# First keys loaded as fp32 by SyncE and converted on chip, counters that write the frequencies, and ScalarE's sine table as its first

## The chip, the core and the metric

The kernel runs on one core of one Trainium2 chip. The core has five engines, each with its own in-order queue: TensorE (PE, matrix products; its weight loads are shown as PEld), VectorE (DVE), ScalarE (ACT), GpSimd (POOL) and SyncE (SP). PE writes to PSUM, the others work between PSUM and SBUF, and 16 DMA engines move data between the device's memory and SBUF. Here loads that convert fp32 to bf16 on the way are issued by POOL; SP issues plain copies and transposes. The metric is the time on the device in microseconds (us), as the median of several executions.

## The reference

Eight batches, eight heads, 576 positions of 64 values; the attention uses 128 random features, and its output goes through a gated convolution along the positions.

```python
def phi(x):                                   # x: q or k, scaled by 64 ** -0.25
    proj = np.einsum('bhsd,md->bhsm', x, omega)
    h = proj - np.sum(x * x, axis=-1, keepdims=True) / 2.0
    return np.exp(h - np.max(h, axis=-1, keepdims=True)) / np.sqrt(m)
kv = np.einsum('bhsm,bhsd->bhmd', k_p, v)
num = np.einsum('bhsm,bhmd->bhsd', q_p, kv)
den = np.einsum('bhsm,bhm->bhs', q_p, np.sum(k_p, axis=2))[..., None] + 1e-06
x = heads_joined(num / den)                   # (8, 576, 512)
proj = x @ w_proj                             # (512, 1536): x1, x2, x3
x2_conv = irfft(rfft(x2, axis=1) * rfft(filter_fft, axis=0), axis=1)
out = (x1 * x2_conv * x3) @ w_out             # (8, 576, 512) fp32
```

## The kernel before

Each batch has 512 main positions, four tiles of 128, and 64 left ones; the left ones of two batches share a tile. The attention of a batch turns keys and queries (`kn`, `qn`) with PE, so that the 64 values lie on partitions (`kt`, `qt`), multiplies them with omega (`om2`), and ACT takes the exponentials (`ek`, `eqt`; `ekl`, `eql` for left positions). A factor 1/max of each key goes into the values on DVE (`vc`, `vcl`), PE sums keys with values (`kv`), multiplies queries with it, DVE divides, and the result is turned into `xt`. Then comes the convolution: `fold` makes three combinations of `xt`, PE multiplies them with `wproj` (`project2`), a forward transform (`fwb`, `fwa`, `fwn`), a product with the transformed filter (`spectrum`), the gates x1 and x3, an inverse transform (`gtab`, `gta`, `gns`), and the product with `wout`. All 576 positions are seen as three chunks of 192 (`CH`), so a transform's length is 192 and the frequencies are of three classes.

The transform's tables are made on the chip at the start. `make_residues` (line 562) builds for each partition its frequencies `fr` on DVE, from a counter `pi` that POOL wrote as int32, along with signs `sg`, phases `ph` and masks `mk`; `fs` is `fr` / 576. A second counter `si` (tile `x2`) holds the positions 0 to 383 and is converted to fp32 in `sc` (tile `xf`). For three groups of columns ACT rounds position x frequency / 576 to a whole number (`yt`, an Identity with a scale per partition), DVE makes the remainder (`xt`, fp16) and, for the cosines, its absolute value with `scalar_tensor_tensor`. `sines` (line 666) has ACT take the five sines, into `gtab`, `gta` and `gn`; `tables` (line 683) turns them with PE. ACT holds one table of functions at a time: it loads that of exponentials first, that of sines ahead of the sines, and that of exponentials again.

Loads: SP issues omega; POOL issues every other load, the keys of batch 0 in two parts (`load_main(0, "k", 2, first_constants)`, line 492) with the counters and the identity for the turns between them, then queries, values, left positions, weights and, behind the residues, the filter, whose tiles `yt` are the residues' before.

The order of instructions is not the program's. `nc` is a `Plan`: each call is recorded with a cost (`_cost`, line 197) and a due time, which is worked out backwards from its users and from the constants `PERIOD`, `STRETCH`, `STAY`, `LEAD`, `SHIFT` and `LEAN` at the top; `simulate` (line 276) goes through a model of the engines and queues and issues, engine by engine, the ready call that is due first. So a change of any cost or constant can move every instruction. All instructions stand in the profile under line 390, where the plan issues them, and are told apart by their tiles.

Of the kernel before, what the change touches and what calls it, by code (L numbers as in the profile page):

```python
# [2 lines left out]

# [11 lines left out]
INT32 = mybir.dt.int32  # L15
# [7 lines left out]
PERIOD, STRETCH, STAY = 132.577, 8.076, 3059.83  # L23
LEAD = {
    "cross keys": -1.86, "cross out": 1.89, "cross queries": -0.95, "filter": -1.41,
    "fold": -1.38, "forward": 68.57, "gates": 0.52, "inverse": -1.95, "keys": 5.37,
    "left keys": -0.11, "left out": -0.33, "left queries": 37.06, "load filter": -63.41,
    "load k": -0.23, "load kl": -0.83, "load q": 0.19, "load ql": 1.42, "load v": 0.21,
    "load vl": -0.15, "load w0": -1.83, "load w1": 5.49, "load w2": 1.25, "out": -1.99,
    "queries": -0.43, "residues": 1.48, "rest": 0.66, "sines": 4.41, "start": -115.12,  # L30
    "sums": 37.58, "tables": -1.3, "turn out": -0.79, "turn queries": -0.04, "values": 96.58,
    "zeros": -0.01,
# [3 lines left out]
    ("fold", 0): -6.59, ("fold", 1): 51.34, ("forward", 1): -64.26, ("forward", 6): -65.11,  # L36
    ("forward", 7): -64.2, ("left keys", 2): 46.16, ("left queries", 7): -36.93,
    ("load kl", 0): -35.9, ("load q", 0): 1.17, ("load v", 0): -95.34, ("load v", 1): 95.91,
    ("load vl", 0): -20.54, ("out", 1): 148.99, ("queries", 1): 32.44, ("queries", 6): -10.06,
    ("rest", 1): 255.75, ("rest", 7): 5.08, ("sums", 2): -41.35, ("sums", 6): -35.91,  # L40
    ("sums", 7): -35.42, ("turn out", 1): 6.64, ("turn out", 2): -370.9,
    ("turn queries", 0): -3.89, ("turn queries", 2): 31.07, ("values", 0): -72.86,
    ("values", 1): 308.0, ("values", 2): -98.35,
}
LEAN = {
    ("fold", "DVE"): 3.25, ("forward", "PE"): 23.82, ("gates", "PE"): 78.43,
    ("keys", "PE"): -26.62, ("rest", "DVE"): 4.62, ("rest", "PE"): -3.97, ("start", "POOL"): 0.17,
    ("turn out", "DVE"): 4.04, ("turn queries", "DVE"): 13.21,
}

SIZE = {FP32: 4, INT32: 4, BF16: 2, FP16: 2, mybir.dt.uint32: 4}
# [58 lines left out]
class Plan:  # L110
# [86 lines left out]
    def _cost(self, op, eng, name, outs, ins):  # L197
# [6 lines left out]
        if name == "dma_start":  # L204
            a = out if out.space != bass.MemoryType.DRAM else ins[0]
            run = a.ap[-1][1] * SIZE[a.dtype]
            rows = a.ap[0][1] * self._free(a) // a.ap[-1][1]
            if eng == "POOL":
                op.busy, op.lat = (880.0 if rows > 600 else 720.0), 3300.0
                op.dma = ("SW", rows * max(run, 166) / 198.0)  # L210
            else:
                op.busy, op.lat = 580.0, 2000.0
                op.dma = ("HW", rows * run / 180.0 / (1 if out.space == bass.MemoryType.DRAM else 4))
            return
# [61 lines left out]
    def simulate(self):  # L276
# [16 lines left out]
        dma_free = {"SW": 0.0, "HW": 0.0}  # L293
        lanes = {"SW": [0.0] * 8, "HW": [0.0] * 8}
        for op in ops:
            if not op.deps:
                ready[op.eng].append(op)
        done, turn = [], {"SW": 0, "HW": 0}
        span, used, slow, half, table = 0, 0.0, True, False, "exp"
        while len(done) < len(ops):  # L300
# [46 lines left out]
            elif op.table and op.table != table:  # L347
                table = op.table
                busy, lat = busy + 1283.0, lat + 1283.0
            if op.dma:  # L350
                kind, serve = op.dma
                go = max(dma_free[kind], at + op.lat)
                if kind == "HW" and dma_free["SW"] > at:
                    go += 2500.0
                    if busy > 1000.0:
                        go, busy = go + 6000.0, busy + 4000.0
                dma_free[kind] = go + serve
# [36 lines left out]
def kernel(  # L394
# [87 lines left out]
    pi_ = nc.tile(const, [P, 1], INT32, name="pi")  # L482
    si = nc.tile(hy, [P, 1024], INT32, name="x2", bufs=2)

    def first_constants():
        was, nc.where = nc.where, ("start", 0)
        nc.gpsimd.iota(pi_[:], pattern=[[1, 1]], base=0, channel_multiplier=1)
        nc.gpsimd.iota(si[:, 0 : 2 * CH], pattern=[[1, 2 * CH]], base=0, channel_multiplier=0)
# [3 lines left out]
    load_main(0, "k", 2, first_constants)  # L492
# [69 lines left out]
    def make_residues():  # L562

        sc = nc.tile(hy, [P, 2 * CH], FP32, name="xf", bufs=2)
        pf_ = nc.tile(const, [P, 4], FP32, name="pf")
        fr = nc.tile(const, [P, 4], FP32, name="fr")
        fl = nc.tile(const, [P, 2], FP32, name="fl")
        sg = nc.tile(const, [P, 2], FP32, name="sg")
        ph = nc.tile(const, [P, 3], FP32, name="ph")
        mk = nc.tile(const, [P, 2], FP32, name="mk")  # L570
        ts, tt = nc.vector.tensor_scalar, nc.vector.tensor_tensor
        stt = nc.vector.scalar_tensor_tensor
        p_ = fr[:, 0:1]
        nc.vector.tensor_copy(out=p_, in_=pi_[:])

        ts(out=pf_[:, 1:2], in0=p_, scalar1=63.5, scalar2=None, op0=ALU.is_ge)
        stt(out=pf_[:, 2:3], in0=pf_[:, 1:2], scalar=-64.0, in1=p_, op0=ALU.mult, op1=ALU.add)
        ts(out=mk[:, 1:2], in0=pf_[:, 2:3], scalar1=31.5, scalar2=None, op0=ALU.is_ge)
        ts(out=mk[:, 0:1], in0=mk[:, 1:2], scalar1=-1.0, scalar2=1.0, op0=ALU.mult, op1=ALU.add)
        stt(  # L580
            out=pf_[:, 3:4],
            in0=mk[:, 1:2],
            scalar=-32.0,
            in1=pf_[:, 2:3],
            op0=ALU.mult,
            op1=ALU.add,
        )
        ts(out=fr[:, 1:2], in0=pf_[:, 2:3], scalar1=128.0, scalar2=None, op0=ALU.add)
        ts(out=fr[:, 2:3], in0=pf_[:, 2:3], scalar1=3.0, scalar2=None, op0=ALU.mult)
        ts(out=fr[:, 3:4], in0=pf_[:, 3:4], scalar1=3.0, scalar2=192.0, op0=ALU.mult, op1=ALU.add)  # L590
        ts(out=fl[:], in0=fr[:, 0:2], scalar1=0.5, scalar2=-0.25, op0=ALU.mult, op1=ALU.add)
        ts(out=fl[:], in0=fl[:], scalar1=MAGIC, scalar2=-MAGIC, op0=ALU.add, op1=ALU.add)
        nc.vector.scalar_tensor_tensor(
            out=fr[:, 0:2], in0=fr[:, 0:2], scalar=1.0, in1=fl[:], op0=ALU.add, op1=ALU.add
        )


        ge2 = pf_[:, 1:2].to_broadcast([P, 2])
        ts(out=sg[:], in0=ge2, scalar1=2.0, scalar2=-1.0, op0=ALU.mult, op1=ALU.add)
        ts(  # L600
            out=ph[:, 0:2],
            in0=ge2,
            scalar1=-math.pi / 2,
            scalar2=math.pi / 2,
            op0=ALU.mult,
            op1=ALU.add,
        )
        nc.vector.memset(ph[:, 2:3], math.pi / 2)
        nc.vector.memset(fr[64:65, 2:3], 288.0)
        nc.vector.memset(sg[64:65, 1:2], -1.0)  # L610
        nc.vector.memset(ph[64:65, 1:2], math.pi / 2)
        zb = nc.tile(const, [P, 1], FP32, name="zb")
        nc.vector.memset(zb[:], 0.0)
        mg = nc.tile(const, [P, 1], FP32, name="mg")
        nc.vector.memset(mg[:], MAGIC)
# [932 lines left out]
```

## Time and profile before

| | us |
|---|---|
| median of three runs | 268.56 |
| the three runs | 266.85, 269.07, 268.56 |
| the profiled execution | 267.76 |
| its span, first to last instruction | 265.8 |
| PE busy | 239.2 (90%) |
| DVE busy | 214.7 (81%) |
| ACT busy | 193.9 (73%) |
| POOL busy | 62.6 (24%) |

The granted TensorE clock was 1.000. The span is what the profile covers; the execution's time has another 1.96 us around it. Busy PE is not PE at its peak, since matrix products overlap and their ends are modelled. The profile's timeline gives for each group its start, its busy time, the engine, the operation, `out<-in` by the names of tiles, and in brackets the idle time ahead of it with what ended it. POOLq and SPq stand for those engines' queues that issue DMAs.

### The profile page before, as it was taken

The numbers are of one execution on the slowest core, as the hardware profiler recorded it, in microseconds if no ns is written. First come the engines' busy times: TensorE is split into PE (matmuls) and PEld (weight loads), VectorE is DVE, ScalarE is ACT, GpSimd is POOL, SyncE is SP. The second block draws the span as 40 slices with busy tenths as digits, with TensorE's granted clock in tenths as the row PEclk, the third lists the DMA queues.
The fourth block names the chain that finished last, engine by engine and source line by source line (L and its number), as shares of the span: only waits on it lengthen the run. The fifth ranks groups of instructions, "written<-read, shape, count | busy, mean of one in ns | idle before, by whom it ended". The sixth has DMA issues, their size and how long they took to land.

```text
span 265.8 us, 5693 instructions
## 1 busy us (share of the span) xinstructions
PE 239.2 (90%) x2202; PEld 133.9 (50%) x2202; DVE 214.7 (81%) x481; ACT 193.9 (73%) x304; POOL 62.6 (24%) x86
## 2 busy tenths in 40 slices
PE   0375879999999998998999599999999999999994
PEld 0264547555466465454854254544664554455541
DVE  7889985678888989998889595999979993576880
ACT  1897898469998989987557548996669647746433
POOL 8745633544453534410230000000000000000000
PEclk9999999999999999999999999999999999999999
DMA  6999999999999999799599727743418053302306
GB/s 78 189 196 176 192 219 221 181 168 163 143 160 147 185 154 100 168 171 217 125 154 167 153 59 194 106 158 91 89 36 244 4 108 129 81 20 64 136 0 197
DMA packets 93026, 36.83 MB, mean 139 GB/s; under 512 B 64459, under 2 KB 87496, under 8 KB 93000
## 3 DMA queue, kind: packets, MB, share of 16 engines
q0 software_dynamic: 59616, 17.31, 64.5%
q1 hardware_dynamic: 33240, 19.04, 32.8%
q8 instruction: 17, 0.28, 0.4%
q10 hardware_dynamic: 144, 0.13, 0.1%
q14 instruction: 9, 0.07, 0.1%
HBM read 34.64 MB, written 9.44 MB: 166 GB/s over the span
## 4 chain that ended last, share of the span: by engine, by line
PE 73%; DMA 11%; ACT 6%; DVE 6%; issue 3%; SPq 0%; ACTq 0%; DVEq 0%
PE h L390 58%; PE a L390 11%; DMA yt<-in_moe_filter_fft_dram 5%; DMA out_dram<-osb 5%; PE t L390 4%; ACT eqt L390 2%; ACT osb L390 1%; DVE yt L390 1%; DMA xw<-xr 1%; DVE x L390 1%; DVE vc L390 1%; SPq L390 0%; ACT yt L390 0%; DVE xt L390 0%; DVE vcl L390 0%
## 5 line engine op out<-in xcount | busy, mean ns | idle before, releaser
L390 PE MATMUL h<-xt,wproj 128*128 128x512 bf16 x256 | 61.7, 380 | 0.0
L390 ACT CAST x<-h 128x512 bf16<-128x512 f32 x68 | 40.2, 600 | 24.7 <-PE h L390 23.4
L390 PEld LDWEIGHTS <-wproj 128*128 128x128 bf16 x384 | 31.0, 99 | 26.3 <-issue 2.3
L390 ACT ACTIVATE osb<-h 128x512 f32<-128x512 f32 (+4 forms) x49 | 27.6, 567 | 11.5 <-PE h L390 6.9
L390 ACT ACTIVATE ek<-a 128x1024 bf16<-128x1024 f32 x32 | 32.1, 1047 | 2.6 <-PE a L390 2.5
L390 ACT ACTIVATE eqt<-a 128x1024 bf16<-128x1024 f32 x32 | 32.6, 1051 | 1.2 <-PE a L390 1.1
L390 PE MATMUL h<-wproj,xf 128*128 128x512 bf16 x128 | 31.4, 380 | 0.0
L390 PE MATMUL h<-wout,yt 128*128 128x512 bf16 x128 | 30.9, 379 | 0.3 <-DVE yt L390 0.3
L390 DVE TENSOR_TENSOR x<-h,x 128x512 bf16<-128x512 f32 x32 | 21.9, 685 | 7.3 <-PE h L390 4.3
L390 POOL DMA_DIRECT2D qn<-in_q_dram x26 | 22.9, 892 | 14.1 <-PE t L390 5.1
L390 PEld LDWEIGHTS <-yt 128*128 128x128 bf16 x128 | 12.2, 98 | 14.8 <-DVE yt L390 0.8
L390 PE MATMUL h<-x,fwb 128*128 128x512 bf16 x72 | 18.5, 379 | 0.9 <-ACT osb L390 0.9
L390 PE MATMUL h<-gtab,xs 128*128 128x384 bf16 x64 | 15.6, 325 | 3.6 <-ACT osb L390 2.2
L390 PEld LDWEIGHTS <-xf 128*128 128x128 bf16 x134 | 12.4, 100 | 12.7 <-issue 0.5
L390 DVE TENSOR_TENSOR bt<-h,osb 128x384 f16<-128x384 f32 x32 | 16.9, 552 | 1.6 <-ACT osb L390 0.7
L390 DVE TENSOR_TENSOR xf<-xt 128x1024 bf16<-128x1024 bf16 (+1 forms) x16 | 8.7, 552 | 7.5 <-ACT xt L390 4.5
L390 PEld LDWEIGHTS <-eqt 128*128 128x128 bf16 x256 | 11.2, 98 | 4.9 <-DVE xb L390 0.7
L390 DVE TENSOR_TENSOR xb<-a,rden 128x512 bf16<-128x512 f32 x20 | 13.2, 678 | 0.3
L390 PE MATMUL a<-om,kt 64*128 64x128 bf16 x256 | 11.8, 223 | 1.5 <-ACT ek L390 0.8
L390 PE MATMUL a<-qt,om 64*128 64x512 bf16 x64 | 11.3, 383 | 1.8 <-DVE qt L390 1.2
L390 POOL DMA_DIRECT2D vn<-in_v_dram x8 | 7.2, 902 | 23.3 <-DVE x13l L390 13.5
L390 PE MATMUL a<-kv,eqt 128*128 128x65 bf16 x256 | 12.5, 194 | 0.0
(168 smaller groups left out, 469.0 us busy)
## 6 DMA issues: line engine op xcount, KB each, us to landing
out_dram<-osb SPq DMA_DIRECT2D x24, 256.0 KB, 2.4
vn<-in_v_dram POOLq DMA_DIRECT2D x8, 512.0 KB, 9.0
kn<-in_k_dram POOLq DMA_DIRECT2D x7, 512.0 KB, 7.3
qn<-in_q_dram POOLq DMA_DIRECT2D x24, 128.0 KB, 9.7
sw<-sp SPq DMA_DIRECT2D x16, 128.0 KB, 2.4
wproj<-in_moe_w_proj_dram POOLq DMA_DIRECT2D x3, 512.0 KB, 13.0
qn<-in_q_dram POOLq DMA_DIRECT2D x2, 512.0 KB, 9.9
out_dram<-xf SPq DMA_DIRECT2D x4, 256.0 KB, 2.0
```

The costliest lines, as they stand in the source:

```text
L390: getattr(real, name)(*args, **kw)
```

## The change

The keys' main part of batch 0 is loaded as fp32 in two DMAs which SP issues, into a tile that takes one of the two `ek` buffers; DVE converts four heads to bf16 and ACT the other four. The counters write fp32 directly: 1 + 3 x partition, and for each half of the partitions 385 + 3 x partition and 3 x partition (within the half); a fourth column adds 192 or 96. These are the frequencies `fi`, so the steps that derived them from a partition's number are gone, as is the conversion of the positions. The frequencies of a class stand in another order than before. The absolute value is taken by clearing the sign bit of fp16 values (`bitwise_and` with 0x7FFF), for two of the three groups only on the partitions that hold cosines. A sine of one zero per partition is ACT's first function, recorded after one memset. The plan gets a third kind of DMA for loads of SP ("HL"), its model charges nothing for the first table load, and all its constants are others. `load_main` keeps its arguments `parts` and `between`, which nothing uses any more.

```diff
-PERIOD, STRETCH, STAY = 132.577, 8.076, 3059.83
+PERIOD, STRETCH, STAY = 136.683, 11.625, 60.43
...
-    "forward": 68.57, "gates": 0.52, "inverse": -1.95, "keys": 5.37,
...
+    "forward": 44.43, "gates": 4.35, "inverse": 10.94, "keys": 0.2, "left keys": -50.63,
...
@@ Plan._cost @@
+            elif out.space != bass.MemoryType.DRAM and ins[0].space == bass.MemoryType.DRAM:
+                op.busy, op.lat = 580.0, 1950.0
+                op.dma = ("HL", rows * run / 330.0)
@@ Plan.simulate @@
-        dma_free = {"SW": 0.0, "HW": 0.0}
+        dma_free = {"SW": 0.0, "HW": 0.0, "HL": 0.0}
         lanes = {"SW": [0.0] * 8, "HW": [0.0] * 8}
+        lanes["HL"] = lanes["HW"]
...
-        span, used, slow, half, table = 0, 0.0, True, False, "exp"
+        span, used, slow, half, table = 0, 0.0, True, False, None
...
             elif op.table and op.table != table:
+                if table:
+                    busy, lat = busy + 1283.0, lat + 1283.0
                 table = op.table
-                busy, lat = busy + 1283.0, lat + 1283.0
...
+                if kind == "HL" and dma_free["SW"] > at:
+                    dma_free["SW"] += serve
@@ the kernel's start @@
-    pi_ = nc.tile(const, [P, 1], INT32, name="pi")
-    si = nc.tile(hy, [P, 1024], INT32, name="x2", bufs=2)
+    fi = nc.tile(const, [P, 4], FP32, name="fi")
+    si = nc.tile(hy, [P, 1024], FP32, name="x2", bufs=2)
 
     def first_constants():
         was, nc.where = nc.where, ("start", 0)
-        nc.gpsimd.iota(pi_[:], pattern=[[1, 1]], base=0, channel_multiplier=1)
-        nc.gpsimd.iota(si[:, 0 : 2 * CH], pattern=[[1, 2 * CH]], base=0, channel_multiplier=0)
+        iota = partial(nc.gpsimd.iota, allow_small_or_imprecise_dtypes=True)
+        iota(fi[:, 0:1], pattern=[[1, 1]], base=1, channel_multiplier=3)
+        for r in (slice(0, 64), slice(64, 128)):
+            iota(fi[r, 1:3], pattern=[[-385, 2]], base=385, channel_multiplier=3)
+        iota(si[:, 0 : 2 * CH], pattern=[[1, 2 * CH]], base=0, channel_multiplier=0)
         nc.opaque("POOL", lambda: make_identity(tc.nc, ident[:]), ident[:], 650.0)
         nc.where = was
 
-    load_main(0, "k", 2, first_constants)
+    def first_keys():
+        nc.at("load k", 0)
+        k32 = nc.tile(att, [P, H, NT, D], FP32, name="ek", bufs=2)
+        t_ = nc.tile(nat, [P, H, NT, D], BF16, name="kn", bufs=2)
+        for g in range(2):
+            hs = slice(4 * g, 4 * g + 4)
+            nc.sync.dma_start(
+                out=k32[:, hs].rearrange("p h t d -> p h (t d)"),
+                in_=k[0, hs, 0:SM, :].rearrange("h (p t) d -> p h (t d)", t=NT),
+            )
+        for g in range(2):
+            hs = slice(4 * g, 4 * g + 4)
+            if g == 0:
+                nc.vector.tensor_copy(out=t_[:, hs], in_=k32[:, hs])
+            else:
+                nc.scalar.copy(out=t_[:, hs], in_=k32[:, hs])
+        nat_tiles["k", 0] = t_
+
+    first_keys()
+    first_constants()
@@ make_residues @@
...
+        ts = nc.vector.tensor_scalar
+        fs, ph, kc, mk = (
+            nc.tile(const, [P, n], FP32, name=m) for n, m in ((4, "fs"), (3, "ph"), (1, "kc"), (2, "mk"))
         )
+        mg, zb = (nc.tile(const, [P, 1], FP32, name=m) for m in ("mg", "zb"))
+        nc.vector.memset(zb[:], 0.0)
+        sn = nc.tile(const, [P, 1], FP32, name="sn")
+        nc.scalar.activation(out=sn[:], in_=zb[:], func=AF.Sin)
+        nc.vector.memset(kc[:], 192.0)
+        for r in (32, 96):
+            nc.vector.memset(kc[r : r + 32, :], 96.0)
+        nc.vector.memset(mg[:], MAGIC)
+        nc.vector.memset(ph[:], math.pi / 2)
+        nc.vector.memset(ph[hi64, 0:2], 0.0)
         nc.vector.memset(ph[64:65, 1:2], math.pi / 2)
+        ts(out=mk[:, 0:1], in0=kc[:], scalar1=150.0, scalar2=None, op0=ALU.is_ge)
+        ts(out=mk[:, 1:2], in0=kc[:], scalar1=150.0, scalar2=None, op0=ALU.is_lt)
+        nc.vector.tensor_tensor(out=fi[:, 3:4], in0=fi[:, 2:3], in1=kc[:], op=ALU.add)
+        nc.vector.memset(fi[64:65, 2:3], 288.0)
+        ts(out=fs[:], in0=fi[:], scalar1=1.0 / S, scalar2=None, op0=ALU.mult)
+
+        def unsigned(o, x):
+            ts(
+                out=o.bitcast(UINT16),
+                in0=x.bitcast(UINT16),
+                scalar1=0x7FFF,
+                scalar2=None,
+                op0=ALU.bitwise_and,
+            )
+
+        for c, n, parts in ((0, 2 * CH, 1), (1, 2 * CH, 1), (2, CH, 2)):
             w = nc.tile(hy, [P, 1024], FP32, name="yt", bufs=2)
             r_ = nc.tile(hy, [P, 2, 1024], FP16, name="xt", bufs=4)
+            kk = w[:, 0 : parts * n]
+            r, ra = r_[:, 0, 0 : parts * n], r_[:, 1, 0 : parts * n]
+            for g in range(parts):
                 nc.scalar.activation(
+                    out=kk[:, g * n : (g + 1) * n],
+                    in_=si[:, 0:n],
                     func=AF.Identity,
+                    scale=fs[:, c + g : c + g + 1],
                     bias=mg[:],
                 )
             ts(out=kk, in0=kk, scalar1=-MAGIC, scalar2=-float(S), op0=ALU.add, op1=ALU.mult)
+            for g in range(parts):
                 nc.vector.scalar_tensor_tensor(
+                    out=r[:, g * n : (g + 1) * n],
+                    in0=si[:, 0:n],
+                    scalar=fi[:, c + g : c + g + 1],
+                    in1=kk[:, g * n : (g + 1) * n],
                     op0=ALU.mult,
                     op1=ALU.add,
                 )
+            if c == 0:
+                unsigned(ra, r)
+            else:
+                unsigned(r[lo64], r[lo64])
+            if c == 2:
+                row = r[64:65, 0:n]
+                unsigned(row, row)
             residues[c] = (r, ra)
         residues["phase"] = ph
@@ sines @@
-        sine(ph[:, 0:1], gtab[:, 2, :], residues[1][1])
-        sine(ph[:, 1:2], gta[:], residues[2][1][:, 0:CH])
-        sine(ph[:, 0:1], gn[:], residues[2][1][:, CH : 2 * CH])
+        sine(ph[:, 0:1], gtab[:, 2, :], residues[1][0])
+        sine(ph[:, 1:2], gta[:], residues[2][0][:, 0:CH])
+        sine(ph[:, 0:1], gn[:], residues[2][0][:, CH : 2 * CH])
```

The lines of `make_residues` that were removed are left out of the diff here; they stand in the code above. `tables`, the attention and the convolution are as before.

## The prediction, made before the changed kernel was run

> **What bounds the kernel now.** I read the slices of the page first, then busy times by stretch, then the timeline of the first 45 us, then the loads there.
>
> ```profile
> PE   0375879999999998998999599999999999999994
> DVE  7889985678888989998889595999979993576880
> ACT  1897898469998989987557548996669647746433
> DMA  6999999999999999799599727743418053302306
> ```
>
> Each digit is a fortieth of the span, 6.6 us. PE is full from the seventh slice on; before that it has gaps, while DVE, ACT and DMA are nearly full. The same by stretches:
>
> ```profile
> 0.00:45.00 45.00, 27.46 (x365) 18.97 (x366) 37.47 (x107) 34.58 (x48) 25.39 (x40) 1.00 1.28 180
> 45.00:90.00 45.00, 45.00 (x472) 26.02 (x471) 36.58 (x73) 37.56 (x57) 22.86 (x29) 1.00 1.78 165
> 90.00:150.00 60.00, 57.02 (x553) 31.80 (x551) 53.29 (x112) 45.90 (x73) 14.39 (x18) 1.00 1.28 158
> 150.00:240.00 90.00, 88.09 (x689) 46.18 (x689) 72.09 (x159) 63.79 (x107) 0.00 (x0) 1.00 0.42 102
> 240.00:265.80 25.80, 21.65 (x131) 10.97 (x128) 15.23 (x33) 12.06 (x22) 0.00 (x0) 1.00 0.32 102
> ```
>
> Columns: stretch, length, then busy us of PE, weight loads, DVE, ACT, POOL. PE's idle time is 45 - 27.46 = 17.5 us in the first 45 us, then 0, 3.0, 1.9 and 4.2. So the sum is nearly "front, then PE's work": what brings the front forward shortens the whole, one for one, as long as data keeps up. Where does the front end, and what orders it?
>
> ```profile
> 3.77 0.18 DVE L390 CAST fr<-pi 128x1 f32<-128x1 int32 x1
> 6.67 0.17 DVE L390 TENSOR_SCALAR fs<-fr 128x4 f32<-128x4 f32 x1
> 6.87 1.31 ACT L390 ACTIVATE yt<-xf,mg,fs 128x384 f32<-128x384 f32 x2 [4.85 <-DVE fs L390]
> ...
> 10.17 1.28 ACT L390 ACT_TABLE_LOAD   x1
> ...
> 13.79 1.28 ACT L390 ACT_TABLE_LOAD   x1
> ...
> 16.01 3.98 ACT L390 ACTIVATE ek<-a 128x1024 bf16<-128x1024 f32 x4
> ...
> 42.41 0.69 DVE L390 TENSOR_TENSOR xf<-xt 128x1024 bf16<-128x1024 bf16 x1 [3.27 <-ACT xt L390]
> ```
>
> ACT waits 4.85 us for DVE's frequencies (fs), makes the residues and sines with two table loads around the sines, and reaches the first key exponential of a main tile at 16.01. From there it is close to full (17.14 of 20 us in 15 to 35, 9.06 of 10 in 35 to 45); at the front's end, 42.41, DVE has stood 3.27 us waiting for ACT's xt, and PE's first product with wproj follows at 42.45. ACT, not DVE, is the last of the front. Last, the loads:
>
> ```profile
> 0.74 0.40 SPq L390 DMA_DIRECT2D osb<-in_omega_dram  x1
> 4.29 2.53 POOL L390 DMA_DIRECT2D kn<-in_k_dram  x3
> 8.56 0.59 PE L390 MATMUL t<-ident,kl 128*128 128x128 bf16 x4 [4.25 <-DMA kl<-in_k_dram]
> 11.46 1.01 PE L390 MATMUL t<-ident,kn 128*128 128x128 bf16 x8 [2.31 <-DVE klt L390]
> GB/s 0 29 9 64 183 194 163 197 197 198 196 180 197 199 203 202 179 200 199 208 200 184 106 148 198 181 198 196 193 198 216 197 228 235 232 226 234 219 217 216
> ```
>
> The last line is what the DMA engines wrote, in fortieths of 0 to 45 us. Nothing but omega's 32 KB moves before 3.4 us, and from 4.5 us on it stands near 197 GB/s of bf16. SP is free after 1.14 us, until 31.
>
> **The change part by part.** The sum is made against the profiled execution, 267.76 us (span 265.8 and 1.96 around it); it lies 0.8 below the median, 268.56, so differences are taken off the median.
>
> Frequencies. Removed ahead of fs on DVE: from the cast at 3.77 to fs at 6.84 there are 3.07 us, of which 0.45 are omega's two copies: 2.6 us of one-column operations (about 0.15 each) and the 0.35 cast of the counter. Added: 13 operations, of which only three depend on a counter (tensor_tensor, memset, fs: 0.16 + 0.06 + 0.17 = 0.4); eight memsets (0.06) and two comparisons (0.15), 0.8 together, can stand between 0.92 and 3.7, where DVE clears vcl, eql and hqs, and cost nothing while those clears have time to spare (0.8 otherwise). POOL writes four counters for two: two more at 0.16, 0.3, ahead of whatever load is queued behind them. When can ACT begin? If the counters stay behind the first loads (pi at 2.46, x at 3.89 to 4.39), at 4.39 + 0.4 = 4.8; if they go ahead of them, POOL has 0.16 x 3 + 0.50 = 1.0 from 1.31 on, so 2.3 + 0.4 and a hop, 2.9. Gain 2.1 to 4.0 on 6.87; I take the middle, 3.0, since two rows give both orders and none prefers one.
>
> Sine table. ACT's first load (at 0.74, idle) becomes the sines', and the one at 10.17 goes: -1.28. It is on ACT's path: exponentials follow it. The one-element sine that fetches the table waits for zb alone, a 0.06 memset, in ACT's empty first 4 us: nothing.
>
> Conversion. ACT copies half the keys, 128x1024: +1.04 by the COPY row of qt, which reads PSUM; from SBUF 384 columns took 0.60 to 0.70 against 0.48 to 0.50 from PSUM, so up to 1.24; I take 1.04, as the sines' 0.60 starts 0.5 apart and so overlaps its neighbour. DVE copies the other half: 384 columns of int32 to fp32 took 0.35, 64 columns of fp32 to bf16 0.22; the slope, 0.13 per 320, puts 1024 at 0.6; the 128x1024 bf16 copy from PSUM took 0.68; I take 0.68. DVE has that room: its own net is -2.6 - 0.35 + 1.2 + 0.68, and the four absolute values (0.55, 0.61, 0.41, 0.41 = 2.0) become masks at the tensor_scalar row's 0.25 to 0.27, four of them, 1.0: in all -2.1, before the 3.27 it idles. Of the shorter absolute values ACT's wait of 1.0 us (before its third residue) gets perhaps half back: -0.5.
>
> So the first key exponential moves by -3.0 - 1.28 + 1.04 - 0.5 = -3.7, if the keys are there. PE's own waits allow it: keys are needed about 5 us ahead of the exponentials.
>
> Keys. POOL loses two issues of some 0.84 (2.53 for three), so each later load on its queue may go 1.7 earlier until it meets a full DMA; SP gains two, 0.4 to 0.6 each, with nothing behind them till 31 us. Omega's first packet moved at about 1.8, 1.0 after issue; so the keys' packets begin near 2.2. 1.05 MB of fp32 takes 2.7 us at the 390 GB/s of the final stores (slices of 369 to 410), 3.6 at the 290 which mixed queues reached at 97 us: both halves there by 5 to 6 us, against 9.8, where PE took the first transposed keys. Beside that, POOL's queue is shorter by 0.52 MB, 2.66 us at 197 GB/s; what the fp32 stream takes from it after 3.4 us comes off: 1.0 to 2.7 remain. PE's first wait, 4.25 for kl at 8.5, stays POOL's, but the main keys can be turned ahead of it.
>
> One rule speaks against this: the Trainium skill, "SBUF — State Buffer", section "Who interferes with whom", says that a VectorE copy in its two-port mode locks GpSimd out, so POOL can't write descriptors. The trace doesn't show it: at 19.54 POOL's issue of ql took 0.70 with the kt copy beside it, 0.68 at 22.17 without. By the rule the sum would lose the conversion's length once; by the row nothing. A second one, "DMA: Bandwidth & Descriptors", section "Rules for kernel authors", holds that spreading DMAs over issuing engines buys no bandwidth, as all share 16 engines; so only the empty first microseconds are won, which is what the sum counts.
>
> **Sum.** ACT allows -3.7, the loads -1.0 to -2.7 where they bind. PE waited for a load only once in the front (kl, 4.2), so I stay nearer to ACT: -3.3. After 45 us the planner gives a new order: its constants all differ, and no row shows that order. There PE idles 4.9 (3.0 + 1.9) ahead of the last stretch; a new order could save most of it or add as much; I take 0. Forecast 268.56 - 3.3 = 265.2, own range 263.7 to 266.4.
>
> **The rivals.**
> *Loads bind.* The front is ready sooner, but q, v, the filter and wproj come at 197 GB/s as before, and the gain is the 0 to 2 us that the queue gets. For: DMA's nines up to 90 us, POOL's waits for earlier loads between 17 and 45. Against: ACT's 4.85 and table loads are no load's doing. 268.56 - 1.0 = 267.6 (266.6 to 268.6).
>
> *Late keys block ACT: slower.* ACT's and DVE's queues run in order. If ACT's conversion is planned ahead of the residues and the fp32 keys share the engines with v and kl, at 150 GB/s (half of the mixed 290), the second half lands at 2.2 + 7.0 = 9.2; ACT copies till 10.3, and its residues start there, not at 6.87: +3.4, less the table load 1.28, plus what kl and v lose to the stream, 0.9 (half of 1.7). +3.0: 271.6 (269.8 to 273). It decides once the second half lands after about 6.9 (a copy's 1.04 later ACT loses what the table load gave). For: SP's small loads beside a full queue at 31 to 40 us took 5.4 to 6.1 to land. Against: the engines are empty when these start.
>
> *More than the front.* The new order also removes ACT's waits for stores (4.3, two of them on the chain, near 118 and 142 us) and PE's 3.1 us wait for osb: -3.3 - 3.7 = 261.5 (259.5 to 263).
>
> That the change doesn't do what it says is slight: ACT's table could be loaded twice still if an exponential were planned between sines; that costs 1.28 and lies in the forecast's own range.
>
> **How the numbers follow.** Forecast 0.5, loads bind 0.2, late keys 0.2, more 0.1. A measurement can tell about 1% (the three times run from 266.85 to 269.07): below 265.9 or above 271.2. Of the forecast's 0.5, 0.41 is below 265.9; with 0.1, faster 0.51. Late keys above 271.2: 0.14. The rest, 0.35, within 1%. The range 261 to 271 leaves out 0.04 of "more" and 0.15 of "late keys".
>
> **What would show it.** Right: two table loads, one at the start; ACT's first residue between 2.9 and 4.8; first main key exponential near 12.3; transposes of kn by 7; wproj's first product near 39; afterwards the same busy PE. The loads rival: first exponential early, but PE idle until wproj or q lands, its first product at 41 or later. Late keys: ACT or DVE idle before ek's copy, released by in_k_dram. More: PE idle under 2 us in 90 to 240. What would make me wrong: an order after 45 us that idles PE much more or less than 4.9 us, which nothing in the trace before can tell.

## The result, and the profile after

The changed kernel takes **275.3 us** (median of four runs, 274.62 to 277.27) against 268.57 for the kernel before beside it (266.85 to 269.07): the ratio is 1.0283, with a 95% interval of 1.0219 to 1.0347, so it is slower. Its profiled execution took 275.79 us with a span of 273.6, against 267.76 and 265.8. Ratios here and below leave disturbed runs out, so they are not exactly quotients of the medians.

The slices of the page of the changed kernel, 6.84 us each:

```profile
PE   0476699999955999999999999999999999999994
ACT  4998468859970798988693695989668637646533
PEclk9999869999995999999999999999999999999999
DMA  7999999999999994989259992964215703401405
```

PE's row has a hole at the twelfth and thirteenth slice (75 to 89 us), where before it was at 9. ACT's has a 0 there as well, while DMA is at 9. PEclk, the clock that TensorE was granted, falls to about half in the thirteenth slice and lower than 9 in the fifth and sixth. The same by stretches (columns as in the prediction: busy us of PE, weight loads, DVE, ACT, POOL, then clock, DMA share and GB/s):

```profile
0.00:45.00 45.00, 27.70 (x336) 17.97 (x339) 35.18 (x96) 33.86 (x46) 25.55 (x42) 0.92 1.33 195
45.00:90.00 45.00, 37.93 (x366) 22.75 (x368) 27.94 (x56) 31.86 (x49) 19.07 (x25) 0.93 1.69 154
90.00:150.00 60.00, 58.98 (x616) 34.25 (x623) 54.01 (x116) 47.98 (x75) 13.29 (x16) 1.00 0.98 130
150.00:240.00 90.00, 89.26 (x697) 46.32 (x707) 72.10 (x162) 66.58 (x110) 3.50 (x4) 1.00 0.60 123
240.00:273.60 33.60, 28.95 (x167) 14.84 (x169) 21.55 (x46) 15.58 (x29) 0.00 (x0) 1.00 0.26 82
```

PE's idle time is 17.3 us in the first 45 (17.5 before), then 7.1 (before 0), 1.0 (3.0), 0.7 (1.9) and 4.7 (4.2). So the front was not won, the middle was lost, and 90 to 240 us became denser by 3.1 us, which doesn't make up for it. The 0.92 in the first stretch is a clock of 0.50 from 32.2 to 39.05 us, which the profiled execution of the kernel before did not have, so the two fronts were not run at the same clock. What opens the hole? PE's timeline there, and the chain of waits at the same place:

```profile
78.48 0.39 PE L396 MATMUL a<-qt,om 64*128 64x512 bf16 x2
85.26 0.58 PE L396 MATMUL t<-ident,kl 128*128 128x128 bf16 x4 [6.38 <-DMA kl<-in_k_dram]
```

```profile
72.32 1.77 POOL qn L396 x2
74.73 10.39 DMA kl<-in_k_dram
85.84 2.20 PE a L396 x40
```

PE stands 6.38 us for the left keys `kl` of batches 4 and 5. The load itself was under way for 10.39 us. POOL's queue, and the loads issued from 72 to 76 us with their median time to landing in us:

```profile
63.71 0.88 POOL L396 DMA_DIRECT2D kn<-in_k_dram  x1 [4.63 <-PE t L396]
67.81 0.87 POOL L396 DMA_DIRECT2D vn<-in_v_dram  x1 [3.21 <-DVE vc L396]
71.46 2.63 POOL L396 DMA_DIRECT2D qn<-in_q_dram  x3 [2.78 <-PE t L396]
74.06 1.40 POOL L396 DMA_DIRECT2D kl<-in_k_dram  x2
```

```profile
qn<-in_q_dram POOLq DMA_DIRECT2D x4, 128.0 KB, 10.5
kl<-in_k_dram POOLq DMA_DIRECT2D x2, 64.0 KB, 10.5
```

The two small `kl` loads stand behind a value load (512 KB) and three query loads (128 KB each) and take as long as these to land. A transpose of `kn` into `kt` that SP issued at 68.55 uses the same DMA engines meanwhile. From 74 to 78 us SP's queue (hardware_dynamic) and POOL's (software_dynamic) moved, in packets, MB and share of the 16 engines' time:

```profile
q1 hardware_dynamic: 1514, 0.39, 95.0%
q0 software_dynamic: 453, 0.18, 36.0%
```

In the kernel before `kl` was issued at 65.16, ahead of the value load (66.89) and the queries (71.08), and turned only at 94.55:

```profile
65.16 1.37 POOL L390 DMA_DIRECT2D kl<-in_k_dram  x2 [1.30 <-PE t L390]
94.55 0.39 PE L390 MATMUL t<-ident,kl 128*128 128x128 bf16 x4
```

ACT at the start:

```profile
3.80 1.28 ACT L396 ACT_TABLE_LOAD   x1 [3.80 <-DVE ph L396]
5.10 1.30 ACT L396 ACTIVATE yt<-x,mg,fs 128x384 f32<-128x384 f32 x2
6.42 1.28 ACT L396 ACT_TABLE_LOAD   x1
7.72 0.20 ACT L396 ACTIVATE sn<-zb 128x1 f32<-128x1 f32 x1
7.83 1.03 ACT L396 CAST kn<-ek 128x1024 bf16<-128x1024 f32 x1
...
12.39 1.28 ACT L396 ACT_TABLE_LOAD   x1
13.68 1.02 ACT L396 ACTIVATE ekl<-a 128x1024 bf16<-128x1024 f32 x1
14.93 1.99 ACT L396 ACTIVATE ek<-a 128x1024 bf16<-128x1024 f32 x2 [0.23 <-PE a L396]
```

There are three table loads, not two. The sine of the zero is recorded first, but the plan issued it behind the first two residues, and these Identities fetched a table that doesn't have the sine. The plan could not see the difference: its `_cost` gives a table to exponentials and sines alone, none to an Identity. So "sines' table is ScalarE's first" did not come true in this order.

### The profile page after: what moved, and what is told of

Its sections match the earlier page's. It is cut to its first block, busy times and chain, and to the rows that moved or that the text cites. A ratio compares the mean times of both kernels' runs of the same rounds, so it can differ in the third digit from the quotient of the medians.

```text
span 273.6 us, 5664 instructions
## 1 busy us (share of the span) xinstructions
PE 242.8 (89%) x2171; PEld 136.1 (50%) x2202; DVE 210.8 (77%) x473; ACT 195.9 (72%) x306; POOL 61.4 (22%) x86
## 4 chain that ended last, share of the span: by engine, by line
PE 67%; DVE 15%; ACT 6%; DMA 5%; issue 3%; POOL 1%; SPq 0%; DVEq 0%; ACTq 0%
PE h L396 51%; PE a L396 12%; PE t L396 4%; DMA kl<-in_k_dram 4%; DVE h L396 2%; DVE vcl L396 2%; DMA sw<-sp 1%; ACT ek L396 1%; DVE vc L396 1%; DVE x L396 1%; DVE xf L396 1%; DVE xs L396 1%; DVE qt L396 1%; DVE xb L396 1%; POOL qn L396 1%
## 5 line engine op out<-in xcount | busy, mean ns | idle before, releaser
L396 PE MATMUL h<-xt,wproj 128*128 128x512 bf16 x243 | 60.5, 380 | 1.2 <-DVE x L396 0.4
L396 ACT CAST x<-h 128x512 bf16<-128x512 f32 x68 | 40.3, 597 | 27.5 <-PE h L396 26.0
L396 ACT ACTIVATE eqt<-a 128x1024 bf16<-128x1024 f32 x32 | 32.0, 1040 | 2.6 <-PE a L396 2.6
L396 ACT ACTIVATE ek<-a 128x1024 bf16<-128x1024 f32 x32 | 31.5, 1039 | 0.9 <-PE a L396 0.7
L396 PE MATMUL h<-wproj,xf 128*128 128x512 bf16 x121 | 30.4, 379 | 0.9 <-DVE xf L396 0.4
L396 PE MATMUL a<-qt,om 64*128 64x512 bf16 x64 | 12.0, 410 | 1.1 <-ACT ek L396 0.5
L396 PE MATMUL a<-kv,eqt 128*128 128x65 bf16 x256 | 11.7, 194 | 1.3 <-DVE xb L396 0.9
L396 PE MATMUL a<-vc,ek 128*128 128x65 bf16 x256 | 12.6, 204 | 0.2 <-DVE vc L396 0.2
## 6 DMA issues: line engine op xcount, KB each, us to landing
qn<-in_q_dram POOLq DMA_DIRECT2D x2, 512.0 KB, 10.5
```

The lines of the kernel that those rows point to most:

```text
L396: getattr(real, name)(*args, **kw)
```

## The experiments

In all of them only the order of issue, the constants or the parts named are changed, unless it is said otherwise; every stage's work is done. Two theories stood against each other. **Order**: the parts of the change are worth what they are, and the new order puts single instructions in bad places. **Parts**: a part itself (the fp32 stream, the conversions) hurts.

### One load's place, and the sine's

The changed kernel with one move each. The plan's finished order is edited before it is issued:

```diff
@@ e1_kl_ahead @@
+    ops = ahead(ops, lambda o: is_(o, "POOL", "load kl", 4), lambda o: is_(o, "POOL", "load q", 4))
@@ e2_sine_head @@
+    first = [o for o in ops if o.where == ("residues", 0) and o.name.split()[1].startswith(("zb", "sn"))]
+    ops = first + [o for o in ops if o not in first]
```

> The changed kernel, with POOL's two loads of kl for batches 4 and 5 issued ahead of the four qn loads of batch 4 instead of behind three of them; nothing else is moved. Theory 'late load': PE's 6.4 us wait for kl near 79 us goes, and with it the half clock from 83 to 90 us, which cost about 2.5 us more: 275.3 - 6 to 9 = 266 to 269, mean granted clock 0.987. Rival 'parts' (the fp32 keys and their conversions hold the front up, the wait only shows it): PE then waits for qn or vn instead and the time stays above 273.

> The changed kernel, with the memset of zb and the one-element sine issued first on DVE and ACT, so that ACT loads the sines' table in its empty first microseconds; two table loads, not three. Theory 'ACT binds the front': the load at 6.42 goes and the first exponential of main keys comes 1.3 us earlier, 13.6 instead of 14.9; if all of that reaches the end, 274.0. Rival 'the front is bound elsewhere' (late loads, half clock): same time within 0.5 us, 275.3.

Moving `kl` ahead of the queries gave 1.0106 (1.0047 to 1.0164), 269.21 us, just above the 266 to 269 expected, so more than half of the loss is in this place. `kl` was issued at 72.62 and landed in 7.1 us, with the value load still ahead of it, and PE still waited:

```profile
80.39 0.38 PE L415 MATMUL t<-ident,kl 128*128 128x128 bf16 x4 [2.35 <-DMA kl<-in_k_dram]
```

The sine at the head gave 1.0233 (1.0183 to 1.0283), 0.5% below the changed kernel, which is not clear of noise by itself since the intervals overlap. There are two table loads, and the first main key exponential comes at 13.85 instead of 14.93. Most of the wait for `kl` stayed (4.96 us of 6.38).

### Constants swapped

```diff
@@ e3_before_consts: the changed kernel @@
-PERIOD, STRETCH, STAY = 136.683, 11.625, 60.43
+PERIOD, STRETCH, STAY = 132.577, 8.076, 3059.83
...
@@ e4_after_consts: the kernel before @@
-PERIOD, STRETCH, STAY = 132.577, 8.076, 3059.83
+PERIOD, STRETCH, STAY = 136.683, 11.625, 60.43
...
```

> The changed kernel's operations, ordered with the constants of the kernel before. Theory 'order': most of the 6.7 us is the new constants' order, so this one loses the wait for kl and lands between 264 and 270. Rival 'parts': the operations themselves cost the time, 273 or more under either set of constants.

> The operations of the kernel before, ordered with the changed kernel's constants. Theory 'order': slower than before, 271 to 280, with a PE wait of several us for some load between 60 and 90 us. Rival 'parts': as before, 267 to 270.

Both missed: 1.0793 (1.0754 to 1.0832) and 1.0883 (1.0833 to 1.0933), spans of 287.1 and 290.0. In both cases the constants did not suit the other kernel's operations, so this swap says nothing of old against new order. It does say what order alone can cost: 24 us in the kernel before (290.0 for 265.8), several times what any part here is worth.

### The parts in the order of before

To price the parts without a new order, every operation that both kernels have keeps its place of the kernel before, and the new ones are put in by hand (the sine and its memset first, the fp32 loads behind omega on SP, the counters and the residues' new steps where those stood that they replace, the conversions beside the residues). The cut is shortened: `place` sorts the operations by that list.

```diff
@@ e5_old_order: all three parts; e6_only_sine, e7_only_keys, e8_only_counters: one each;
   e11_sine_keys: two @@
-        for op in self.order():
+        ops = place(self.order(), new)     # the order of before, and where the new ones go
+        for op in ops:
```

> All three parts of the change, but every instruction that both kernels have stands in the order of the kernel before; the new ones are put by hand (the keys' DMAs behind omega on SP, counters at the old counter's place, one-element sine first on ACT, conversions where the residues leave room). Theory 'order': the parts themselves gain what they free in the front, 1 to 3.3 us, and the loss of the changed kernel is its order: 0.988 to 0.996 of the kernel before, no PE wait for kl near 79 us, no half clock. Rival 'parts': the fp32 stream and the conversions cost more than they free: 1.005 or more.

> The kernel before in its own order, with one more memset and a one-element sine issued first on DVE and ACT; nothing else. ACT has two table loads, not three. Theory 'ACT binds the front': 1.28 us earlier from the first sine on and at the end, 0.995 of the kernel before. Rival 'DVE or the loads bind': the sines come earlier but wait for DVE's remainders or ek for the keys, 1.000.

> The kernel before in its own order, with only the keys of batch 0 loaded as fp32 by SP (issued behind omega) and converted, half by DVE behind the masks and half by ACT behind its first two residues. Theory 'the stream displaces': POOL's first packets wait until the fp32 stream ends near 6 us, kl is turned no earlier than before (8.5), and since kn is turned behind kl nothing is gained: 0.998 to 1.006. Rival, the prediction's term: POOL's queue is 1.0 to 2.7 us shorter and this reaches the end, 0.990 to 0.996.

> The kernel before in its own order, with only the counters that write frequencies, the shorter residues and the masks for absolute values; three table loads, keys by POOL. Theory 'ACT binds the front': ACT's first residue starts about 2 us earlier (4.9 instead of 6.9) and the first key exponential of a main tile 1 to 2 us earlier: 0.993 to 0.997. Rival 'kl and the keys bind': PE turns kl at 8.5 as before and ek starts at 16: 1.000.

> The kernel before, in its own order, with two of the three parts: the sine of a zero first, and the fp32 keys by SyncE with their two conversions; the counters, residues and absolute values stay as they were. If the parts add up: e6_only_sine 0.9933 times e7_only_keys 0.9972 makes 0.9905, the best of all. If the front's gain is capped by PE's and ACT's order between 14 and 25 us, as the traces of e5_old_order read: 0.993 to 0.996, with the first main key exponential near 14.5 and the first product with wproj near 42.5 to 43.5 all the same.

| | ratio to before (95%) |
|---|---|
| all three parts | 0.9939 (0.9896 to 0.9981) |
| sine first | 0.9933 (0.9889 to 0.9976) |
| fp32 keys by SP | 0.9972 (0.9943 to 1.0001) |
| counters | 1.0006 (0.9977 to 1.0035) |
| sine and keys | 0.9880 (0.9830 to 0.9930) |

No part hurts beyond its interval, so the theory of the parts falls. All three together and the sine came as expected, the counters as their rival had it, and the keys lie between their two expectations. The parts are also small: all three make 0.6%, and the pair without the counters has the lowest ratio of the study, 264.84 us (264.21 to 265.98), though its interval overlaps those of all three and of the sine. The product of the two single ratios, 0.9905, lies inside it. The pair's conversions do not stand where the keys alone have them: ACT's is ahead of the residues, waits 4.03 us for the fp32 keys, and the residues begin at 7.46 instead of 6.87.

The front's gain does not reach the end one for one. ACT in the kernel with all three parts, in the old order:

```profile
14.02 1.02 ACT L1773 ACTIVATE ek<-a 128x1024 bf16<-128x1024 f32 x1
17.05 2.85 ACT L1773 ACTIVATE ek<-a 128x1024 bf16<-128x1024 f32 x3 [2.02 <-PE a L1773]
21.77 3.82 ACT L1773 ACTIVATE ek<-a 128x1024 bf16<-128x1024 f32 x4 [1.86 <-issue]
```

The first exponential is 2.0 us earlier than before (14.02 for 16.01), but the fourth ends at 19.90 for 19.99, the fifth to eighth start 0.5 later (21.77 for 21.27), and the first product with `wproj` starts at 42.38 for 42.45. ACT now waits for PE, and PE's turns of the keys and queries stand where they stood:

```profile
15.42 1.06 PE L1773 MATMUL t<-ident,kn 128*128 128x128 bf16 x8
...
20.22 0.92 PE L1773 MATMUL t<-ident,kn 128*128 128x128 bf16 x8 [1.14 <-DVE kt L1773]
22.04 1.04 PE L1773 MATMUL t<-ident,qn 128*128 128x128 bf16 x8
```

Before, these three were at 15.49, 20.29 and 22.02:

```profile
15.49 1.06 PE L390 MATMUL t<-ident,kn 128*128 128x128 bf16 x8
20.29 0.61 PE L390 MATMUL t<-ident,kn 128*128 128x128 bf16 x8 [1.13 <-DVE kt L390]
```

The second turn takes 0.92 us here and 0.61 before. In this execution the clock was at 0.50 from 20.35 to 23.76, in that of the kernel before it was not. The gain was gone ahead of that; the 0.5 us that the later keys lose can be the clock's.

The pair of sine and keys failed the expectation of a cap (0.993 to 0.996, exponential near 14.5): its first exponential is at 16.01, as before, its first product with `wproj` at 44.98, later than before, and yet its ratio is the lowest. Its profiled execution is the slowest of its six and had the clock at 0.50 from 26.6 to 30.0 and from 40.3 to 43.7, so part of that lateness can be the clock's. Still, "where the front ends", read in one execution, doesn't give this kernel's time. Its idle PE time is 17.7 us up to 45 us (17.5 before) but 1.5 from 90 to 150 (3.0) and 1.0 from 150 to 240 (1.9). These are readings of one execution each; what in the parts shortens the later waits was not tried by itself and stays open.

### The cures added up, and the move reversed

`kl` goes one place further ahead than in the first experiment, in front of the value load of batch 4: alone, and together with the sine at the head. And the kernel before gets the changed kernel's late `kl`.

```diff
@@ e12_kl_alone and e9_kl_and_sine: the changed kernel @@
+    ops = ahead(ops, lambda o: is_(o, "POOL", "load kl", 4), lambda o: is_(o, "POOL", "load v", 4))
@@ e9_kl_and_sine besides @@
+    ops = first + [o for o in ops if o not in first]
@@ e10_kl_behind: the kernel before @@
+    qs = [o for o in ops if is_(o, "POOL", "load q", 4)]
+    later = ops[ops.index(qs[2]) + 1 :]
+    ops = ahead(ops, lambda o: is_(o, "POOL", "load kl", 4), lambda o: o is later[0])
```

> The changed kernel with both cures: POOL's two kl loads of batches 4 and 5 go ahead of the value load of batch 4 (one place further ahead than in e1_kl_ahead, where PE still waited 2.4 us for them), and the zero and its sine go first on DVE and ACT. Order theory: the two cures add up, 1.0106 less the 0.5% that the sine gave, so ratio 1.000 to 1.008, PE's wait for kl near 75 to 85 under 1 us, two table loads, no half clock after 45 us. Rival, a third trouble further back takes the room (the front's gain is lost before 45 us as in e5_old_order): still 1.010 or more, with PE idle over 17 us in the first 45. Second rival, the parts' own gain comes through: under 0.995.

> The changed kernel with the two kl loads ahead of the value load of batch 4, as in e9_kl_and_sine, and nothing else: the sine of a zero stays where the plan put it, so three table loads. If the load's place carries most and the sine 0.5% to 0.7% as it did in e2_sine_head and e6_only_sine: ratio 0.996 to 0.999, PE's wait for kl after 45 us under 1 us, no half clock there. If the one place further ahead than in e1_kl_ahead changes nothing and the sine carries the rest: 1.008 to 1.013, with a wait of 2 us or more near 80 us still there.

> The kernel before with one edit: its two kl loads of batches 4 and 5 stand behind three of the four query loads of batch 4 on POOL's queue, as the changed kernel has them; nothing else moves. If the late load is what costs: PE waits 4 us or more for kl between 75 and 90 us, the granted clock halves right there, and the ratio is 1.012 to 1.025. If the late load hurts only the changed kernel's order (here PE has other products ready that are queued ahead of the turns of kl): under 1.006, with no half clock near 80.

With nothing but the two loads' place changed, the ratio is **0.9996** (0.9965 to 1.0026), next to the 0.996 to 0.999 expected: the whole loss of 2.8% is gone. With the sine at the head as well it is **0.9919** (0.9883 to 0.9955), 265.83 us, below the 1.000 to 1.008 that adding the cures was to give, as the second rival had it. That version is faster than both kernels, as are all three parts, the sine, and sine and keys in the old order. The stretch of 45 to 90 us of the first of these, its turn of `kl`, which waits for nothing, and the loads issued from 72 to 76 us:

```profile
45.00:90.00 45.00, 44.70 (x488) 26.27 (x484) 34.87 (x71) 38.15 (x59) 21.01 (x28) 1.00 1.52 159
```

```profile
79.01 0.40 PE L415 MATMUL t<-ident,kl 128*128 128x128 bf16 x4
```

```profile
kl<-in_k_dram POOLq DMA_DIRECT2D x2, 64.0 KB, 2.7
```

`kl` is issued at 73.65 here, after 8.86 us of waiting for PE to release its tile, so only 0.4 us earlier than in the changed kernel. What changed is what is ahead of it and beside it: it lands in 2.7 us instead of 10.5 (7.1 with the value load alone ahead). POOL issued no load from 64.8 to 73.65 here, and SP's transpose was through by 74 (0.30 MB from 71.5 to 74 us, nothing from 74 to 78), so the DMA engines were free as well. The price was that of the way to landing, not of the time of issue. How much of it the bytes ahead on POOL's queue made, and how much SP's transpose beside them, was not separated.

PE idles 0.3 us there instead of 7.1, at a full clock instead of 0.93, and the span is 265.5 instead of 273.6, 8.1 us less. The wait makes 6.25 us of that, the distance between the two turns of `kl` (85.26 for 79.01). The rest is the clock: it is at 0.50 from 83.40 to 90.25 in the changed kernel, and the products behind the wait run slower. The same ones in the changed kernel and with both cures:

```profile
85.64 0.26 PE L396 MATMUL a<-vcl,ekl 128*128 128x65 bf16 x1
85.92 0.25 PE L396 MATMUL a<-vcl,ekl 128*128 128x65 bf16 x1
```

```profile
78.19 0.20 PE L418 MATMUL a<-vcl,ekl 128*128 128x65 bf16 x1
78.36 0.19 PE L418 MATMUL a<-vcl,ekl 128*128 128x65 bf16 x1
```

They follow each other every 0.28 us instead of 0.17. The first product behind the stretch, in the changed kernel and with `kl` alone put ahead:

```profile
91.33 0.81 PE L396 MATMUL h<-x,fwb 128*128 128x512 bf16 x2
83.18 0.81 PE L415 MATMUL h<-x,fwb 128*128 128x512 bf16 x3
```

Here the changed kernel lags by 8.15 us, so the half clock cost 8.15 - 6.25 = 1.9. At the last products the lag is 8.1 (266.67 for 258.57): nothing behind this place adds to the loss or takes from it.

The reversal in the kernel before costs nothing, 1.0006 (0.9967 to 1.0045), against the first expectation. POOL and PE in it:

```profile
72.23 2.64 POOL L411 DMA_DIRECT2D qn<-in_q_dram  x3 [3.32 <-PE t L411]
74.84 1.40 POOL L411 DMA_DIRECT2D kl<-in_k_dram  x2
```

```profile
65.62 0.40 PE L411 MATMUL t<-ident,kl 128*128 128x128 bf16 x4
95.70 0.39 PE L411 MATMUL t<-ident,kl 128*128 128x128 bf16 x4
```

The loads are as late as in the changed kernel and behind the same others (8.0 us to landing), but PE turns that `kl` at 95.70 (94.55 in the kernel before), 21 us behind the issue. The changed kernel's PE had it queued next at 78.9, less than 5 us behind the issue, with 10.5 to landing. So the new order moved both ends towards each other: the load back by 9 us, its use forward by 16. That the old order bears the late load is shown; that the new one would bear it with PE's turn put back was not tried.

## Why the prediction was wrong, by its steps

**The order after 45 us.** This is the step that failed: "a new order could save most of it or add as much; I take 0", around 4.9 us of idle PE. The new order added 8.1 us in one place, 6.25 of wait and 1.9 of half clock, and undoing that place alone takes 1.0283 to 0.9996. Both the 0 and its bounds came from PE's idle time. But what a misplaced load costs is its way to landing, 10.5 us here, less the lead that PE's order leaves it, 4.8, and the slower clock behind that, and PE's idle time before says nothing of any of these. The prediction said itself that no row of before could tell the new order; they only hinted at the danger: DMA at 9 up to 90 us, and POOL waiting there for tiles with loads behind it.

**The frequencies.** ACT's first residue was to move from 6.87 to 2.9 to 4.8. It came at 5.10, behind ACT's first table load, which ran at 0.74 in the kernel before and here waited for DVE until 3.80. With the sine at the head that load is at 0.74 again and the residue at 3.84, as forecast. In the old order with the counters alone the load waited for `fs` until 5.21, the residue came only at 6.50, and the part brought nothing (1.0006); with the sine first besides (all three parts) it came at 5.24. So the size of the term was right where the table was out of the way; that the first load stays at 0.74 was assumed without a reason.

**The sine's table.** The prediction counted -1.28 us, called it slight that the change doesn't do what it says, and saw the risk in an exponential between sines. It was an Identity: three loads came instead of two, all on ACT's path, where in the kernel before two were. So the term came as +1.28. With the sine at the head, two came, one of them in ACT's empty time, and the first exponential went from 14.93 to 13.85; the time fell by 0.5% (1.3 us) beside the late load, which is not clear of noise, and by 0.8% (2.1 us) without it (0.9996 to 0.9919, intervals apart). So -1.28 was about the right price of something that did not happen.

**The conversion.** ACT's share took 1.03 us (1.04 forecast) and DVE's 0.69 (0.68). Both sizes were right. In DVE's net the 0.35 of the counter's cast is counted twice (it lies in the 2.6), so it is -1.7 and not -2.1; nothing hung on that. The row from which the prediction took that a DVE copy costs POOL nothing, 0.70 for 0.68, shows a copy that reads PSUM. The conversion reads SBUF, and the same filter load took POOL longer to issue beside it (at 8.46 with all three parts in the old order) than in the kernel before:

```profile
8.50 1.16 POOL L1773 DMA_DIRECT2D yt<-in_moe_filter_fft_dram  x1 [1.26 <-DVE xt L1773]
9.95 0.84 POOL L390 DMA_DIRECT2D yt<-in_moe_filter_fft_dram  x1 [1.50 <-DVE xt L390]
```

In the changed kernel it was 0.95 for `vl` at 8.68, beside the conversion, after 0.75 for the one before. So the trace doesn't clear POOL of this price; it is 0.2 to 0.3 us in these two places and too small to decide anything here.

**The first exponential.** In the changed kernel it moved by 1.1 us, from 16.01 to 14.93, where 3.7 were forecast. With both cures it stands at 13.86, 2.15 us ahead of before. Of that the first residue gave 3.0 and the table load 1.28, as forecast, less the conversion's 1.05. The 1.5 that are missing of the 3.7 are in ACT's waits, which the forecast let shrink by 0.5: the 0.99 ahead of the third residue is gone, but ACT now waits 1.73 for DVE's last residue, and 0.18 and 0.22 for its conversion's data and the first product. The kernel with both cures:

```profile
5.32 1.05 ACT L418 CAST kn<-ek 128x1024 bf16<-128x1024 f32 x1 [0.18 <-DMA ek<-in_k_dram]
...
8.17 0.60 ACT L418 ACTIVATE gtab<-xt,ph 128x384 bf16<-128x384 f16 x1
10.49 0.46 ACT L418 ACTIVATE x<-xt,ph 128x192 bf16<-128x192 f16 x1 [1.73 <-DVE xt L418]
```

**The keys.** Their packets ran from 2.2 to 6.2 us, 4.0 us for 2.7 to 3.6 forecast: slowly up to 3.5 us, then at 372 to 386 GB/s at the peak. The other half failed: POOL's queue was to gain 1.0 to 2.7 us and lost instead. In the old order with the keys alone POOL issued its first load at 1.46, as before (1.44), but its first packet came at 5.42 instead of 3.17. The first `kl` was turned at 10.46 instead of 8.56, and since PE has `kl` queued first, the main keys were turned no earlier (11.55 for 11.46). In the changed kernel `kl` is POOL's first load and was turned at 7.98 and the main keys at 10.98, where the prediction looked for them by 7. It had seen that the main keys "can be turned ahead of it"; no order here did so.

**"What brings the front forward shortens the whole, one for one".** This fell too. In the old order, 2.0 us won at 14 us were gone by 20, at PE's queue. In the changed kernel's own order the front's -3.3 did not come either: with the late load cured and nothing else the ratio is 0.9996, which is -0.1 us (-0.9 to +0.7). The first product with `wproj`, looked for near 39, came at 45.52, behind the half clock at 32.2 to 39.05.

**The rivals.** "Loads bind" (267.6) named the right kind of bound, for the wrong load and in the wrong place. "Late keys block ACT" (271.6) did not happen: ACT's wait for the fp32 keys is 0.18 us above, and none in the changed kernel; only in the pair, with the conversion put ahead of the residues by hand, was it 4.03. "More than the front" (261.5) nearly came true in its size: it expected 3.7 us less idle PE behind the front, and from 90 to 240 us there are 3.1 less in the changed kernel too (1.8 for 4.9); the hole ahead of that hides it, and what shortens these waits stays open. The slower outcome came by a mechanism that was not among the rivals. The forecast's 265.2 is close to the 265.83 of the kernel with both cures, but that is luck, since other terms make it. Against before, PE idles there 1.3 us less up to 45 us (16.3 for 17.5) and 3.2 less from 90 to 240 (1.7 for 4.9), 0.9 more between, and is busy 1.4 longer: -1.3 + 0.9 - 3.2 + 1.4 = -2.2, the 263.6 of its span for 265.8.

## What to carry to other kernels

When a change makes a planner issue a new order, the order is a term of its own and can outweigh every part: look up each load's issue and first use in the new queues, and where its lead is shorter than the loads ahead of it and the transfers beside it need, count the difference and the slower clock behind it. Price the parts by putting them into the old order by hand, and cure single places in the new one before judging either. A move that is meant to make something first has to be checked in the issued order, not in the program's.

## What the runs showed of the hardware

**The clock and PE's work.** In these fourteen traces the granted clock is 1.00 or 0.50 and changes only at the ends of pieces of 3.41 us. In the changed kernel it was at 0.50 from 83.40 to 90.25 and from 32.2 to 39.05. PE had done nothing for 4.5 us when the first of these began. A gap of 2.35 us at the same place (the first experiment) brought no fall, one of 4.96 us (the sine at the head) did. The Trainium skill, "TensorE: Matmul & The Clock Gate", section "Part 1: The HAM clock gate", puts the fall behind an idle window of some 3.4 us, which agrees with these three. The fall at 32.2 does not fit: in the 3.4 us ahead of it PE was busy for 1.7. Taken over all traces, an idle piece is not needed: each of the 31 falls came behind a piece in which PE was busy for 2.06 us or less, and each return to 1.00 behind one with 3.19 or more. Of the 961 pieces at 1.00 that were not followed by a fall, 947 had more than 2.06 us and 14 had 1.48 to 2.06. So little work goes with every fall, but doesn't bring one every time; what decides in between no run here shows. The falls in the front are not the change's own, since the front of the kernel before is as thin (27.46 us busy of 45) and other executions of it had a mean clock of 0.987.

The records begin only at 15.2 us in the changed kernel and at 17.4 before. Ahead of that the profile prints 1.00, but eight turns of `kn` took 1.01 us at 11.46 before, and 0.61 at 20.29: PE worked at the slower pace at first.

**Tables of functions.** The same skill, "ScalarE: Activation LUTs", section "Table sets: the hidden batching unit", says that cheap functions are in every set as filler and names the identity among them. Here that did not help: an Identity as the first function fetched a set without the sine (at 3.80 us), and the sine fetched another (at 6.42). Only with the sine first were there two loads, and the Identities behind it fetched none. Nor did the first load always use ACT's empty time. It ran at 0.74 ahead of the sine, and ahead of an Identity that read only what DVE had written (the kernel before). Ahead of an Identity that read POOL's counter too it ran at 3.80 and 5.21 (the changed kernel, and the counters alone). What holds it there was not tried.

**A stream of another queue at the start.** One MB of plain copies from SP, 386 GB/s at its peak, held POOL's first converted packets back by 2.25 us (5.42 for 3.17), with POOL's first issue at 1.46 and 1.44 (the keys alone in the old order, and the kernel before).
